# Sharing the first pass over the weights among three chunks of tokens instead of two

## The chip, the cores and the metric

The kernel runs on one core of a Trainium2 chip. The metric is the device time of one execution in microseconds: 958.51 as the median of three runs before the change (957.35 to 958.92). TensorE is written PE below, VectorE DVE, ScalarE ACT, GpSimd POOL, and SyncE, which only issues transfers here, SP.

## The reference

Windowed attention, and behind it a two-layer network with a rational function between the layers:

```python
scores = q @ k.T / sqrt(64)           # 8 batches, 8 heads, 576 positions, 64 wide
mask = (rel >= 0) & (rel < 64)        # rel = query position - key position
attn = softmax(where(mask, scores, -1e9))
x = (attn @ v) as (4608 tokens, 512)
h = x @ w_in                          # 512 x 2048
P = a0 + a1*h + a2*h^2 + a3*h^3
Q = 1 + |b0|*|h| + |b1|*h^2
out = (P / (Q + 1e-6)) @ w_out        # 2048 x 512
```

The weights come in double precision, everything else in float32.

## The kernel before

**Chunks and steps.** The 4608 tokens are nine chunks of 512 (c0 to c8), and the 2048 hidden columns are 16 weight tiles of 128. A step is one chunk with one tile: 12 matmuls for h (`products` of `plan_gate`, L688, called F1 below), a gate on ACT, POOL and DVE (L691 to L733: six DVE operations, of which the first two, L703 and L706, are the last to read h), and 12 matmuls that add to the chunk's output in four PSUM banks (`products` of `plan_out`, L771, called F2). Each product is made of three float32r matmuls: high times low, low times high, high times high. F2 of a step is due three steps (`LAG`) behind its F1. There are 144 steps. h has two PSUM buffers, the gate's temporaries two, its results three.

**Decoding.** Each weight tile comes as double-precision words and is decoded on the chip into a high and a low float32r tile, once for w_in and once for w_out (`plan_decode`): a load of 512 KB, ACT L393, POOL L397, DVE L401 and L406, ACT L417, DVE L420. The decoded tiles stay in SBUF for all chunks. Tiles 8 to 15 are put together in two PSUM banks, b0 and b1.

**Attention.** Each chunk's x is made by four units, one for two heads (`plan_unit`): loads of q, k and v, scores on PE (L527), maxima on DVE, exponentials on ACT, a product on POOL (L589), transposes on PE (L594), the product with v (L608, into one of the two h buffers), and x as high and low tile (L613, L617). c0 and c1 have SBUF buffers of their own, in room that weight tiles take later; from c2 on, a unit uses the buffers `kt`, `w_c`, `vt`, `sm`, `pT` and the banks b0 and b1, which decoding uses too. From chunk `JOIN` on, b0 and b1 are read as one tile. Units of chunks after `PF` have the next unit's scores right behind the product with v.

**Phases.** `phases` (L325) lists (chunk, first tile, tile behind the last). c0 goes over tiles 0 to 7, c1 over all 16, c0 again over 8 to 15, and then each chunk over all. So a tile's decoding is due at its first use: tiles 0 to 7 at steps 0 to 7, tiles 8 to 15 at steps 16 to 23. x has two slots of SBUF. Where a chunk has a phase to come, its partial output goes to memory (`send`, L785) and is added later (L779). If the chunk's x slot has been given away meanwhile, `kept` and `plan_reload` write x to memory and read it back; before the change no chunk needs that.

**Order.** `Plan.order` (L72) simulates the engines with a cost for each operation, and the instructions are written in the order of its start times. Of the operations on an engine that could start within 0.02 us of the first, the one of the lowest rank goes. Ranks are in steps: a gate's is its step, a w_in decode's `need - LI`, its load's `LD` less, a unit's the step that `AH` puts it ahead. `N1` is taken off the rank of L703 and L706. The dictionaries `TILE_AT`, `FETCH_AT`, `UNIT_AT`, `GATE_AT`, `OUT_AT` shift single ranks. SP issues an operation once PE has come within `ahead` steps of its rank.

Of the kernel before, what the change touches and what calls it, by code (L numbers as in the profile page):

```python
# [45 lines left out]
class Plan:  # L46
# [25 lines left out]
    def order(self):  # L72
# [22 lines left out]
        while len(done) < len(self.ops):  # L95
            best = None
            for e in ENGINES:
                able = []
                for op in ready[e]:
                    if e == "SP" and op.rank > now + self.ahead:  # L100
                        continue
                    if any(not slots[s.pool] for s in op.takes):
                        continue
                    t = max([free[e], op.ready + op.late] + [min(slots[s.pool]) for s in op.takes])
                    if op.port:
                        t = max(t, port["POOL" if e == "DVE" else "DVE"])
                    if e == "SP":
                        t = max(t, bus - 2.5)
                    able.append((t, op))
                if not able:  # L110
                    continue
                t0 = min(t for t, _ in able)
                t, op = min(((t, op) for t, op in able if t <= t0 + 0.02), key=lambda x: (x[1].rank, x[0], x[1].n))
                if best is None or t < best[0]:
                    best = t, op
            t, op = best
            for s in op.takes:
                slots[s.pool].remove(min(slots[s.pool]))
                held[s] = len(s.uses)
            cost, e = op.cost, op.engine  # L120
            if e == "PE":
                t += self.TURN.get((last, op.kind), 0.0)
                done_us, at = 0.0, t
                while done_us < cost - 1e-6:
                    w = int((at - self.OFFSET) // self.WINDOW)
                    while seen < w:
                        part = load.get(seen, 0.0) / self.WINDOW
                        fast = part > (0.465 if fast else 0.85)
                        seen += 1
                    slow = 1.0 if fast else self.SLOW[op.kind]  # L130
                    step = min((cost - done_us) * slow, (w + 1) * self.WINDOW + self.OFFSET - at + 1e-6)
                    load[w] = load.get(w, 0.0) + step
                    at += step
                    done_us += step / slow
                cost, last = at - t, op.kind
                now = max(now, op.rank)
            if op.port:
                if e == "DVE" and t == port["POOL"]:
                    cost = 0.55
                port[e] = t + (cost - 0.15 if e == "DVE" else op.port)  # L140
            op.start, op.end = t, t + cost
            if e == "SP":
                bus = max(t, bus) + op.cost
                op.end = bus + 2.0
                free[e] = t + 0.12
            elif e == "PE":
                free[e] = op.end
                op.end += self.DRAIN[op.kind]
            else:
                free[e] = op.end - self.TAIL[e]  # L150
            ready[e].remove(op)
            done.append(op)
            for s, n in list(held.items()):
                if op in s.uses:
                    held[s] -= 1
                    if not held[s]:
                        slots[s.pool].append(max(o.end for o in s.uses) + self.LATENCY)
                        del held[s]
            for o in then.get(op, ()):
                left[o] -= 1  # L160
                if not left[o]:
                    o.ready = max(x.end - self.DRAIN[x.kind] if x.engine == o.engine == "PE" else
                                  x.end + (0.111 if x.kind == "R" and o.engine == "DVE" else self.LATENCY) for x in o.after)
                    ready[o.engine].append(o)
# [16 lines left out]
def swa_rational_ffn(ctx: ExitStack, tc: tile.TileContext, qT, kT, v, w_in, w_out, a, b, out):  # L181
# [7 lines left out]
    NF = DFF // P  # L189
# [12 lines left out]
    tmp = ctx.enter_context(tc.tile_pool(name="tmp", bufs=2))  # L202
    gp = ctx.enter_context(tc.tile_pool(name="gp", bufs=3))
# [90 lines left out]
    w_out_v = w_out.rearrange("(fc p) e -> p fc e", p=P)  # L294

    EC = 2
    PF = 3
    HA = H
    LI, LO = (4, 1.5), (2, 1.5)
    C0R, AH = -12.0, (2, 2, 3.0)  # L300
    TILE_AT = {12: -0.5, 17: -0.5, 18: -2, 20: -1.5, 4: 0.25}
    FETCH_AT = {(0, 2): -0.5, (2, 0): -2, 12: 1}
    UNIT_AT = {(0, 1): 2, (1, 0): -1.5, (2, 0): -0.5}
    GATE_AT = {13: 1, 18: 1.25, 22: -1, 31: 0.25, 33: -0.75, 34: -2, 36: -1}
    OUT_AT = {25: -2, 5: -3}
    UN, GT, F2R, OUTR, N1, SG, LD = 0.3, 0.02, 0.5, -0.5, 0.0, 0, 2.0
    KEEP = 4
    PT_DVE = ((0, 0), (0, 1))
    XH_DVE = ((0, 0), (0, 1))
    LENT = ((0, 1),)  # L310
    MASK_US = 4.8
    PSC = 8
    JOIN = 3
    WC = 2
    ps_b = Early(tc, "ps_b", 1, space=bass.MemoryType.PSUM)
    banks = [ps_b.pool.tile([P, 512], F32, name=f"bank{z}") for z in range(2)]
# [2 lines left out]
    def join():  # L319
        ps_b.close()  # L320
        pool = ctx.enter_context(tc.tile_pool(name="ps_a", bufs=1, space=bass.MemoryType.PSUM))
        span.append(pool.tile([P, 2, 512], F32, name="banks"))
        banks[:] = [span[0][:, z, :] for z in range(2)]

    phases = [(0, 0, 8), (1, 0, NF), (0, 8, NF)]  # L325
    phases += [(c, 0, NF) for c in range(1 + max(c for c, _, _ in phases), NCH)]
    steps = [(c, i) for c, i0, i1 in phases for i in range(i0, i1)]
    total = len(steps)
# [21 lines left out]
    for s, (c, i) in enumerate(steps):  # L350
        need.setdefault(i, s)

    plan = Plan({"w_st": 3, "w_c": WC, "b0": 1, "b1": 1, "kt": 1, "e0": 4, "e1": 2, "sme": 2, "pTe": 2, "sm": 2, "vt": 1, "pT": 1, "h": 2,
                 "tmp": 2, "gp": 3, "o0": 1, "o1": 1, "o2": 1, "o3": 1}, 5.0)
    ready_in, ready_out = {}, {}

    parts = tiles(H, NF)
# [18 lines left out]
    def plan_decode(i, src, his, los, rank, z):  # L376
        in_psum = i >= PSC
        n = 2 * i + z
        plan.shift = TILE_AT.get(n, 0.0)
        home = HOMES[n % len(HOMES)] if n < FROM else "w_st"  # L380
# [41 lines left out]

        plan.shift += FETCH_AT.get(n, 0.0)
        o = plan.add("SP", 1.6, rank - LD, load, uses=[st])
        plan.shift = TILE_AT.get(n, 0.0)
        o = plan.add("ACT", 0.66, rank, scale, [o], [st, sc])
# [20 lines left out]
    def plan_unit(c, hp, rank):  # L447
        early = c < EC
        plan.shift = UNIT_AT.get((c, hp), 0.0)
        if early:  # L450
# [62 lines left out]
        def scores():  # L513
            if c:
                if c >= JOIN and not span:
                    join()
# [12 lines left out]

        joined = c >= JOIN  # L530
        PARTS = [slice(0, NR)] if joined else [slice(z * PR, (z + 1) * PR) for z in range(2)]
# [79 lines left out]
        def x_high():  # L611
            xh[c, hp] = xp.tile([P, CH], F32R, name=f"xh{hp}_{slot_of[first_of[c]]}", bufs=1)
            (nc.vector.tensor_copy if (c, hp) in XH_DVE else nc.scalar.copy)(out=xh[c, hp], in_=u["px"].rearrange("p t s -> p (t s)"))  # L613

# [5 lines left out]
        def link(kind, op):  # L620
            chain[kind] = op
            return op

        r = lambda n: rank + UN * n
        paired = c > PF or c == PF and hp > 0
        ahead = (-2.5 if c > PF else -1 if hp else 2) if c >= PF else 5.5 - hp
        plan.shift += FETCH_AT.get((c, hp), 0.0)
        o = link("load_qk", plan.add("SP", 1.7, r(0) - 2 if early else r(0) + ahead, load_qk, [], [sqk, sq]))
        lv = link("load_v", plan.add("SP", 1.4, r(0) - 1.9 if early else r(0) + ahead + 0.1, load_v, [o], [svt]))
        plan.shift = UNIT_AT.get((c, hp), 0.0)  # L630
        m = [plan.add("PE", 0.51, r(1) - 2, masks, [chain.get("scores")], sps, late=MASK_US if hp == 0 else 0.0, kind="F")] if c == 0 else []
# [18 lines left out]
        link("values", o)  # L650
        oh = plan.add("DVE" if (c, hp) in XH_DVE else "ACT", 0.69 if (c, hp) in XH_DVE else 0.594, r(10), x_high, [o] + free_x.get(c, []), [spx])
        o = plan.add("DVE", 0.688, r(11), x_low, [oh], [spx])
# [24 lines left out]
    def plan_gate(s):  # L677
        c, i = steps[s]
        plan.shift = GATE_AT.get(s, 0.0)
        sh, st, sg = Slot("h"), Slot("tmp"), Slot("gp")  # L680
# [74 lines left out]
    def plan_out(s):  # L755
# [3 lines left out]
        d, sg = gs.pop(s)  # L759
        plan.shift = OUT_AT.get(s, 0.0)  # L760
        if first:
# [114 lines left out]
```

## Time and profile before

| what | value |
|---|---|
| median of three runs | 958.51 us |
| the profiled execution: its own time | 959.0 us |
| the profiled execution: span of the trace | 957.0 us |
| PE busy | 934.6 us, 98% of the span |
| DVE busy | 791.6 us, 83% |
| ACT busy | 669.8 us, 70% |
| POOL busy | 330.7 us, 35% |
| granted TensorE clock, mean | 0.993 |

The span goes from the first to the last instruction. An engine is busy while an instruction of it runs; matmuls overlap, so PE is read from its gaps and from the spacing of starts. Register, branch and DMA-issuing instructions are not counted.

### The profile page before, as it was taken

Reading aid. Unit: us, or ns where it says so; the run is one execution under the profiler, and the core shown is the slowest. Engines: PE = TensorE matmul, PEld = TensorE weight load, DVE = VectorE, ACT = ScalarE, POOL = GpSimd, SP = SyncE. Lnnn points to the kernel's source line nnn. Section 1 sums busy time; section 2 is a strip of 40 time slices with the busy share of each in tenths; the row PEclk is TensorE's granted clock in tenths of the full one; section 3 lists DMA queues with packets and bytes.
Section 4 is the critical chain, followed back from the end, with each engine's and each line's share of the span. In section 5 each row is a group of like instructions: output and inputs, shape, how many; then the busy total and the mean of one; then the engine's idle time right before and its main releaser. Section 6 shows DMA issues by size and latency. Waiting matters only on the chain.

```text
span 957.0 us, 16313 instructions
## 1 busy us (share of the span) xinstructions
PE 934.6 (98%) x6068; PEld 752.0 (79%) x6068; DVE 791.6 (83%) x1198; ACT 669.8 (70%) x1477; POOL 330.7 (35%) x227
## 2 busy tenths in 40 slices
PE   7798999999999999999999999999999999999998
PEld 4576778778888888888888888888888888888886
DVE  5999999999797977887787787887879778777775
ACT  6788777778767577676776677667676676756564
POOL 4756355533323233233323233233132332322221
PEclk9799999999999999999999999999999999999999
DMA  8831323122421112101211121111211121001001
GB/s 301 280 108 45 121 99 113 66 91 85 137 98 44 44 44 71 58 2 54 76 44 44 43 76 54 45 48 48 92 46 46 46 78 35 1 1 45 0 1 45
DMA packets 39103, 66.47 MB, mean 69 GB/s; under 512 B 5616, under 2 KB 22256, under 8 KB 39024
## 3 DMA queue, kind: packets, MB, share of 16 engines
q1 hardware_dynamic: 39024, 65.43, 20.9%
q8 instruction: 48, 0.79, 0.3%
q14 instruction: 31, 0.25, 0.1%
HBM read 54.92 MB, written 10.49 MB: 68 GB/s over the span
## 4 chain that ended last, share of the span: by engine, by line
PE 82%; DVE 11%; issue 2%; DMA 2%; ACT 1%; POOL 0%; SPq 0%; ACTq 0%; DVEq 0%; POOLq 0%
PE o L771 37%; PE h L688 36%; PE ps_x L608 3%; PE banks L527 3%; PE banks L594 2%; DMA w_st<-w_in 2%; DVE gh L720 2%; DVE num L703 1%; DVE gl L733 1%; DVE num L728 1%; DVE u L724 1%; DVE num L706 1%; DVE bank L401 1%; DVE w_c L401 1%; ACT sm L577 1%
## 5 line engine op out<-in xcount | busy, mean ns | idle before, releaser
L710 POOL TENSOR_TENSOR u<-u,ah 128x512 f32<-128x512 f32 x144 | 203.1, 1410 | 422.9 <-ACT u L700 294.9
L688 PE MATMUL h<-xl,wi_h 128*128 128x512 f32 x576 | 230.5, 400 | 4.8 <-DVE num L706 3.2
L771 PE MATMUL o<-wo_h,gl 128*128 128x512 f32 x576 | 231.9, 403 | 0.3 <-ACT ob L783 0.2
L688 PE MATMUL h<-xh,wi_l 128*128 128x512 f32 x576 | 227.8, 396 | 0.0
L688 PE MATMUL h<-xh,wi_h 128*128 128x512 f32 x576 | 227.5, 395 | 0.0
L771 PE MATMUL o<-wo_h,gh 128*128 128x512 f32 x576 | 226.7, 393 | 0.0
L771 PE MATMUL o<-wo_l,gh 128*128 128x512 f32 x576 | 225.8, 392 | 0.0
L713 ACT ACTIVATE ah<-u 128x512 f32<-128x512 f32 x144 | 91.0, 633 | 114.8 <-POOL u L710 114.7
L720 DVE SCALAR_TENSOR_TENSOR gh<-num,a_sb,ah 128x512 fp32r<-128x512 f32 x144 | 111.3, 773 | 49.9 <-ACT ah L716 48.5
L694 ACT ACTIVATE ah<-h 128x512 f32<-128x512 f32 x144 | 85.9, 597 | 81.9 <-PE h L688 56.8
L703 DVE TENSOR_TENSOR num<-num,h 128x512 f32<-128x512 f32 x144 | 98.3, 683 | 45.5 <-ACT num L697 45.3
L688 PEld LDWEIGHTS h<-xl,wi_h 128*128 128x128 f32 x576 | 108.5, 188 | 34.0 <-DVE num L706 4.8
L771 PEld LDWEIGHTS o<-wo_h,gl 128*128 128x128 f32 x576 | 108.2, 188 | 26.9 <-issue 3.1
L688 PEld LDWEIGHTS h<-xh,wi_l 128*128 128x128 f32 x576 | 108.5, 188 | 26.1
L688 PEld LDWEIGHTS h<-xh,wi_h 128*128 128x128 f32 x576 | 108.7, 189 | 24.8
L771 PEld LDWEIGHTS o<-wo_h,gh 128*128 128x128 f32 x576 | 108.1, 188 | 25.2
L771 PEld LDWEIGHTS o<-wo_l,gh 128*128 128x128 f32 x576 | 108.3, 188 | 22.6
L589 POOL TENSOR_TENSOR sm<-sm,rs 128x1024 f32<-128x1024 f32 x36 | 69.8, 1940 | 159.4 <-ACT ah L694 88.1
L728 DVE SCALAR_TENSOR_TENSOR num<-num,a_sb,u 128x512 f32<-128x512 f32 x144 | 115.9, 806 | 2.3
L700 ACT ACTIVATE u<-ah,b_sb 128x512 f32<-128x512 f32 x144 | 117.3, 815 | 0.0
L724 DVE SCALAR_TENSOR_TENSOR u<-u,gh 128x512 f32<-128x512 f32 x144 | 106.2, 738 | 7.1
L697 ACT ACTIVATE num<-h,a_sb 128x512 f32<-128x512 f32 x144 | 111.9, 777 | 0.0
(80 smaller groups left out, 1095.3 us busy)
## 6 DMA issues: line engine op xcount, KB each, us to landing
out<-ob SPq DMA_DIRECT2D x35, 256.0 KB, 2.0
w_st<-w_in SPq DMA_DIRECT2D x16, 512.0 KB, 5.2
w_st<-w_out SPq DMA_DIRECT2D x16, 512.0 KB, 4.1
vt<-v SPq DMA_DIRECT2D x8, 448.0 KB, 5.7
vt<-v SPq DMA_DIRECT2D x8, 384.0 KB, 3.3
vt<-v SPq DMA_DIRECT2D x8, 320.0 KB, 3.9
q<-qT SPq DMA_DIRECT2D x8, 256.0 KB, 4.8
kt<-kT SPq DMA_DIRECT2D x8, 256.0 KB, 4.3
```

Source lines behind the costliest of these rows:

```text
L589: nc.gpsimd.tensor_tensor(out=sm, in0=sm, in1=u["rs"].unsqueeze(2).broadcast_to([P, NR, P]), op=ALU.mult)
L688: nc.tensor.matmul(h, w[i][:, cc, :], x[c, cc], start=n == 0, stop=n == 3 * NCC - 1)
L694: nc.scalar.activation(d["ah"], d["h"], AF.Abs)
L697: nc.scalar.activation(d["num"], d["h"], AF.Identity, scale=a_sb[:, 3:4], bias=a_sb[:, 2:3])
L700: nc.scalar.activation(d["u"], d["ah"], AF.Identity, scale=b_sb[:, 1:2], bias=b_sb[:, 0:1])
L703: nc.vector.tensor_tensor(out=d["num"], in0=d["num"], in1=d["h"], op=ALU.mult)
L710: nc.gpsimd.tensor_tensor(out=d["u"], in0=d["u"], in1=d["ah"], op=ALU.mult)
L713: nc.scalar.activation(d["ah"], d["u"], AF.Ln, bias=QADD)
L720: nc.vector.scalar_tensor_tensor(out=d["gh"], in0=d["num"], scalar=a_sb[:, 0:1], in1=d["ah"], op0=ALU.add, op1=ALU.mult)
L724: nc.vector.scalar_tensor_tensor(out=d["u"], in0=d["u"], scalar=QADD, in1=d["gh"].bitcast(F32), op0=ALU.add, op1=ALU.mult)
L728: nc.vector.scalar_tensor_tensor(out=d["num"], in0=d["num"], scalar=a_sb[:, 0:1], in1=d["u"], op0=ALU.add, op1=ALU.subtract)
L771: nc.tensor.matmul(acc[t], g[:, ts], w[i], start=first and n == 0, stop=last and n == 2)
```

## The change

The list of phases becomes: c0 over tiles 0 to 7, c1 over 0 to 9, c2 over all 16, c1 over 10 to 15, c0 over 8 to 15, and then c3 to c8 over all. Three things follow from existing code. Tiles 8 and 9 are due at steps 16 and 17, tiles 10 to 15 at steps 28 to 33. c2's attention is due at step 18 instead of 32, and c2's x takes the slot of c0's, so c0's eight x tiles (256 KB each) go to memory and come back for step 40; c1 has a partial output that is stored and added as c0's is. Chunk 3 is read with two separate banks and without pairing (`JOIN` and `PF` go from 3 to 4). The planner's constants are other ones.

```diff
-                t, op = min(((t, op) for t, op in able if t <= t0 + 0.02), key=lambda x: (x[1].rank, x[0], x[1].n))
+                t, op = min(((t, op) for t, op in able if t <= t0 + 0.05), key=lambda x: (x[1].rank, x[0], x[1].n))
...
-    PF = 3
+    PF = 4
     HA = H
-    LI, LO = (4, 1.5), (2, 1.5)
-    C0R, AH = -12.0, (2, 2, 3.0)
-    TILE_AT = {12: -0.5, 17: -0.5, 18: -2, 20: -1.5, 4: 0.25}
-    FETCH_AT = {(0, 2): -0.5, (2, 0): -2, 12: 1}
-    UNIT_AT = {(0, 1): 2, (1, 0): -1.5, (2, 0): -0.5}
-    GATE_AT = {13: 1, 18: 1.25, 22: -1, 31: 0.25, 33: -0.75, 34: -2, 36: -1}
-    OUT_AT = {25: -2, 5: -3}
-    UN, GT, F2R, OUTR, N1, SG, LD = 0.3, 0.02, 0.5, -0.5, 0.0, 0, 2.0
+    LI, LO = (1.5, 1.25), (2, 4)
+    C0R, AH = -12, (5, 0, 2)
+    TILE_AT = {22: 0.25, 7: -0.25}
+    FETCH_AT = {17: -0.5}
+    UNIT_AT = {(1, 1): -2, (2, 1): 0.5}
+    GATE_AT = {0: -1, 17: -0.25, 20: -0.25}
+    OUT_AT = {}
+    UN, GT, F2R, OUTR, N1, SG, LD = 0.1, 0.1, 0.25, -1.75, 3.5, 0, 4
     KEEP = 4
     PT_DVE = ((0, 0), (0, 1))
-    XH_DVE = ((0, 0), (0, 1))
+    XH_DVE = ((0, 0),)
...
-    JOIN = 3
+    JOIN = 4
...
-    phases = [(0, 0, 8), (1, 0, NF), (0, 8, NF)]
+    phases = [(0, 0, 8), (1, 0, 10), (2, 0, NF), (1, 10, NF), (0, 8, NF)]
...
-                 "tmp": 2, "gp": 3, "o0": 1, "o1": 1, "o2": 1, "o3": 1}, 5.0)
+                 "tmp": 2, "gp": 3, "o0": 1, "o1": 1, "o2": 1, "o3": 1}, 3.0)
```

The last number is `ahead`.

## Rows read from the trace of the kernel before

**Rows 1.** The page: busy time of the engines over the span, and the granted TensorE clock in 40 slices, in tenths of full speed.

```profile
PE 934.6 (98%) x6068; PEld 752.0 (79%) x6068; DVE 791.6 (83%) x1198; ACT 669.8 (70%) x1477; POOL 330.7 (35%) x227
...
PEclk9799999999999999999999999999999999999999
```

**Rows 2.** Busy time of each engine in five stretches. The columns: the stretch and its length, then PE, PE's weight loads, DVE, ACT and POOL with their instructions, the granted clock, the DMA share and GB/s.

```profile
17.60:26.60 9.00, 4.58 (x80) 3.84 (x80) 7.80 (x16) 6.51 (x27) 7.18 (x5) 1.00 0.96 345
26.60:94.30 67.70, 58.73 (x513) 46.02 (x513) 65.07 (x102) 56.70 (x143) 43.55 (x27) 0.90 0.43 140
94.30:111.10 16.80, 16.80 (x72) 13.63 (x73) 16.80 (x28) 11.58 (x19) 4.52 (x3) 1.00 0.25 95
111.10:199.40 88.30, 87.72 (x375) 69.60 (x374) 87.79 (x139) 65.73 (x110) 45.74 (x31) 1.00 0.27 90
199.40:252.00 52.60, 52.60 (x514) 42.02 (x513) 47.21 (x80) 44.12 (x130) 18.65 (x12) 1.00 0.38 118
```

**Rows 3.** The same view for single lines, between 111.1 and 199.4 us: F1's matmuls (L688; PE and its weight loads), F2's (L771), a gate's last DVE operation (L733, one for a gate) and a decode's last (L420, one for half a tile pair). The fifth row is L733 between 199.4 and 252 us, the sixth L420 between 26.6 and 94.3.

```profile
111.10:199.40 88.30, 44.96 (x183) 33.97 (x183) 1.00 0.27 90
...
111.10:199.40 88.30, 47.46 (x192) 35.64 (x191) 1.00 0.27 90
...
111.10:199.40 88.30, 10.86 (x16) 1.00 0.27 90
...
111.10:199.40 88.30, 10.21 (x15) 1.00 0.27 90
...
199.40:252.00 52.60, 5.14 (x7) 1.00 0.38 118
...
26.60:94.30 67.70, 9.11 (x13) 0.90 0.43 140
```

**Rows 4.** PE in order of time between 47 and 95 us: start, length, line, operation, and in brackets the idle time before it and what ended it. The second and third row are two matmuls in a row of the same F1.

```profile
47.81 0.50 PE L688 MATMUL h<-xl,wi_h 128*128 128x512 f32 x1 [2.23 <-DVE num L706]
...
49.45 0.63 PE L688 MATMUL h<-xh,wi_l 128*128 128x512 f32 x1
49.87 0.63 PE L688 MATMUL h<-xl,wi_h 128*128 128x512 f32 x1
...
59.25 1.15 PE L608 MATMUL ps_x<-pT,vt 128*64 128x64 f32 x32 [0.89 <-DVE num L706]
...
62.60 1.15 PE L608 MATMUL ps_x<-pT,vt 128*64 128x64 f32 x32 [0.61 <-DVE xl L617]
...
79.22 0.49 PE L688 MATMUL h<-xl,wi_h 128*128 128x512 f32 x1 [0.75 <-DVE num L706]
...
88.58 1.15 PE L608 MATMUL ps_x<-pT,vt 128*64 128x64 f32 x32 [0.55 <-ACT bank L393]
...
94.29 0.50 PE L688 MATMUL h<-xl,wi_h 128*128 128x512 f32 x1 [1.61 <-DVE xl L617]
```

**Rows 5.** DVE in order of time: the last operation of two gates in a row. Nine operations start from the first to before the second: six of gates and three of decoding.

```profile
149.35 0.67 DVE L733 TENSOR_TENSOR gl<-num,ah 128x512 fp32r<-128x512 f32 x1
...
154.93 0.67 DVE L733 TENSOR_TENSOR gl<-num,ah 128x512 fp32r<-128x512 f32 x1
```

**Rows 6.** Groups of instructions: the DVE operation that makes the gate's high part between 26.6 and 94.3 us, and the same between 94 and 200 us. Busy time and mean ns of one stand behind the bar, then the idle time before. Last, one such operation in the chain of waits: start, length.

```profile
L720 DVE SCALAR_TENSOR_TENSOR gh<-num,a_sb,ah 128x512 fp32r<-128x512 f32 x6 | 7.2, 1207 | 0.5 <-ACT ah L716 0.5
...
L720 DVE SCALAR_TENSOR_TENSOR gh<-num,a_sb,ah 128x512 fp32r<-128x512 f32 x19 | 14.5, 762 | 0.1
...
53.80 2.31 DVE gh L720
```

**Rows 7.** Groups of instructions between 199.4 and 252 us: the maxima of the attention, one for a unit.

```profile
L568 DVE TENSOR_REDUCE nmx<-sm 128x8 f32<-128x1024 f32 x5 | 6.1, 1213 | 0.1
```

**Rows 8.** SP's issue of the first weight load, and the loads of one unit in the list of DMA issues: size, and us to landing.

```profile
8.05 0.33 SPq L387 DMA_DIRECT2D w_st<-w_in  x1
...
vt<-v SPq DMA_DIRECT2D x8, 448.0 KB, 5.7
...
q<-qT SPq DMA_DIRECT2D x8, 256.0 KB, 4.8
kt<-kT SPq DMA_DIRECT2D x8, 256.0 KB, 4.3
```

**Rows 9.** The chain of waits between 200 and 260 us, in order of time: start, length, what. All of it is PE. The first row is the first scores of c2, the last c2's first F1.

```profile
201.96 1.03 PE bank L527 x32
...
221.13 1.08 PE ps_x L608 x32
222.21 0.90 PE o L771 x3
223.11 0.87 PE bank L594 x8
...
233.27 0.69 PE o L771 x3
...
250.28 1.03 PE banks L527 x32
251.31 0.89 PE o L771 x3
252.20 2.79 PE h L688 x12
```

**Rows 10.** Single lines over the whole span: who waited for the copies that empty the output banks (L783; us, times), and the landing time of the 256 KB stores (L790).

```profile
  PE o L771: 0.2, 1
...
DMA to landing us min/median/max: 1.7/2.0/3.3
```

## The prediction

> **What bounds the kernel now.** I read the shares of the engines first [rows 1]: PE at 98% of the span with the clock down only in the first two fortieths, so nearly all that can be won lies early. The stretches [rows 2] then show three regimes. Up to 94.3 us PE is held: between 26.6 and 94.3 it is busy 58.73 of 67.70, at a mean clock of 0.90, beside a DVE that is busy 65.07. From 94.3 to 199.4 us both are full: PE 104.5 of 105.1, DVE 104.6. From 199.4 PE alone is full. A loss behind 94 us could therefore only be a new one, and a gain has to come from the 9.0 us that PE stands before it and from the clock.
>
> What PE waits for there is in its order of time [rows 4]: twice L706, which gives back an h buffer (2.23 and 0.75 us), and four times for the attention of c1, its product with v or the h buffer that this product holds (0.89, 0.61, 0.55, 1.61). After the 2.23 us the next F1 runs part of its way with starts 0.43 us apart (49.45 to 49.87), where the full stretch has 87.72 us for 375 matmuls [rows 2], 0.234 each: the lower clock level. Some 8 of the 12 matmuls have it, 8 x 0.20 = 1.6 us. Together these are 6.6 + 1.6 = 8.2 us.
>
> Why could the order of the work not simply be made better there? DVE's prices say it. Between two ends of gates lie 154.93 - 149.35 = 5.58 us and nine operations [rows 5], 0.62 each: a gate (six) is 3.72 us, half a tile pair of decoding (three) 1.86. Check: between 111.1 and 199.4 us end 16 gates and 15 halves [rows 3], 16 x 3.72 + 15 x 1.86 = 87.4, and DVE was busy 87.79. A step is 24 matmuls on PE, 24 x 0.234 = 5.61. So for steps 8 to 23, with tiles 8 to 15 due in them, DVE needs 16 x 3.72 + 16 x 1.86 = 89.3 us and PE 16 x 5.61 = 89.8. There is no slack: had PE come to step 8 earlier, DVE would have made it wait afterwards. DVE's work up to 199 us is what sets the end, and PE's early gaps only show it.
>
> **The change part by part.**
>
> *Decoding later, c2 earlier.* Out of steps 8 to 23 go six tiles, 12 halves or 22.3 us of DVE; in come four units of c2. Their price: between 199.4 and 252 us DVE is busy 47.21 [rows 2], seven gates take 26.0, and 21.2 are left for four to five units [rows 3, 7], 4.5 each. Steps 8 to 17 then cost DVE 37.2 + 7.4 (two tiles) + 18.0 = 62.6 us, and PE 56.1 + four units of about 3.2 (1.03 + 0.87 + 1.08 and turns [rows 9]) = 68.9. Steps 18 to 33 cost DVE 59.5 + 22.3 = 81.8 and PE 89.8. DVE now has 6 and 8 us to spare, where it had none. By itself this is worth nothing, as PE is full there; it allows the front to be shorter.
>
> *The front.* Three edits use it: N1 = 3.5 puts L703 and L706 ahead of other DVE work, which is the wait of 2.23 and 0.75; c1's units come three steps earlier, into PE's idle time, which is the other four waits; LI = 1.5 decodes w_in tiles later beside them. At most all 8.2 us go. DVE sets a limit: from 26.6 to 111.1 us it does 81.9 us of work, of which about 5 (L703 and L706 of two steps, 2.5, and tile 8's first operations, 2.5) aren't needed by the eighth F2, and it idles 2.6; so the front can be shorter by 5 to 8. At least nothing is won: the order changes and DVE's sum does not. It can also be a loss, priced among the rivals. I take half of 8.2, 4.1 us: the first wait and its clock are cured by N1 alone (3.8), and the rest is shared with what DVE then owes.
>
> *Loads.* The ranks put two units of c1, some 960 KB each [rows 8], ahead of the first weights, issued at 8.05 us now. At 345 GB/s [rows 2] that is 5.6 us. The first F1 comes some 30 us later [rows 4] and DVE has attention to do until then, so I take 0; without this cover 5.6.
>
> *x out and back.* Eight tiles of 256 KB go out and eight come in, 4.2 MB or 12 us at 345 GB/s, while the queues run at 90 to 118 GB/s [rows 2]; a store lands in 2.0 us [rows 10]. It costs no engine anything but SP its issues. Coming back, the loads have from the end of c2's F1 to step 40, six steps or 34 us, for 6.1 + 4 us. Going out, c2's x tiles wait for the stores, and these aren't issued before PE is at step 11 (rank 14, `ahead` 3). I take 0; the upper end is a rival.
>
> *A second partial output.* Four more ACT copies and four more DVE additions (one operation, 0.62 each) lie in slack behind step 18. One more change of the output banks: at all of them together PE waited 0.2 us once [rows 10], so +0.2, between 0 and 0.2.
>
> *c3 unpaired.* Where other products follow scores or a product with v, three matmuls of F2 take 0.89 or 0.90 instead of 0.69 [rows 9]; a pair pays these 0.2 us once, separated ones twice. Three units: +0.6. c3's separate banks make an operation of 1024 columns into two of 512, in the slack of DVE and ACT: 0, or 1 us were it not there.
>
> Sum: -4.1 + 0.2 + 0.6 = -3.3. The profiled execution took 959.0 us (span 957.0), 0.5 above the median of the runs: 955.7 on its scale, 955.2 against the median.
>
> **The rivals.**
>
> *More is won.* With the lead DVE has, N1 lets all of the 8.2 us go: 959.0 - 8.2 + 0.8 - 0.5 = 951.1. For it: the slack of 6 and 8 us. Against it: DVE's limit of 5 to 8, of which N1 itself spends 2.5.
>
> *The front gains nothing.* POOL and DVE get into each other's way: L720 takes 1.207 us in the front and 0.762 later, one of them 2.31 [rows 6]. With LI = 1.5 more decoding lies among the gates. Three more meetings at 2.31 - 0.76 = 1.55 are 4.6 us, which takes the 4.1 away: 959.0 + 0.5 + 0.8 - 0.5 = 959.8; without the meetings but with an order no better, 959.3. Against it: two of c1's POOL products leave the gates' stretch for the time before it. The Trainium skill has a rule for this (SBUF — State Buffer, "Who interferes with whom"): a VectorE instruction with two SBUF inputs contends with a GpSimd instruction that reads SBUF, and the later one waits until the other is done. The length of 2.31 us agrees.
>
> *c2 is late* (slower). Before, from c2's first scores to its first F1 went 252.20 - 201.96 = 50.2 us [rows 9]. Now there are seven steps and four units for it, from step 11, where the stores may go, to step 18: 39.3 + 12.8 = 52 us. The eight stores need 6.1 + 2.0 = 8 of these before the first x tile can be written, and ACT, which writes the x tile, holds gates behind that wait. If the units keep the old pace behind the stores, c2's x is 6 us late. F2 of the three steps before covers up to 8.4 us, but the gates then run dry as well. From the point where the last unit ends more than 8.4 us late, PE stands; I price it at 6 us and two F1 at the lower clock, 2 x 1.6: 955.2 + 9.2 = 964.4. Against it: the old pace was that of a full DVE, and the new stretch has 6 us of slack. The Trainium skill's clock gate rule (TensorE: Matmul & The Clock Gate, "HAM oscillation — how this bites in real kernels") says that matmuls after a long enough wait run at half clock; the rows on the 2.23 us agree, and if the clock stayed up, this rival would be 961.2.
>
> **How the numbers follow.** The forecast gets 0.47, all 8.2 us 0.13, no gain 0.20, c2 late 0.20. From 950.5 to 962.5 us lie the forecast, no gain, most of the better case and the lighter half of the late one, 8 in 10. A run can tell 0.2% from no change, 1.9 us: faster is under 956.6, slower over 960.4. The forecast lies below 956.6 in 0.40 of its 0.47; faster 0.53. No gain gives most of its part to no change: 0.21 with the rest of the forecast. Slower 0.26.
>
> **What would show it.** Right: PE idle before 94 us falls from 9.0 in that stretch to about 5, no PE wait on L706 of over 1 us, the eighth F2 starts 3 to 5 us before 111.1, and PE is full from there on, across c2's first F1 and step 40. DVE has idle time between steps 8 and 34. Wrong: the eighth F2 comes no earlier (no gain), L720 above 1.2 us in the front (the shared port), a PE wait of several us on c2's x or behind a store (c2 late), or one at step 40 on the x read back, for which I have kept nothing.

## The result and the profile after

The changed kernel takes 963.75 us (median of four runs, 962.96 to 964.31), the kernel before 958.71 beside it (957.35 to 959.62). The ratio is 1.0052, with a 95% interval of 1.0037 to 1.0067: slower by 5.0 us, where 3.3 less was forecast. The profiled execution took 963.37 us, its span is 961.6 (957.0 before), its mean granted clock 0.990 (0.993).

The page of the kernel after, the same lines as in [rows 1]:

```profile
PE 936.8 (97%) x6068; PEld 752.4 (78%) x6068; DVE 791.1 (82%) x1209; ACT 672.7 (70%) x1482; POOL 337.5 (35%) x227
...
PEclk8999999999999999999999999999999999999999
```

The stretches of the kernel after, with the columns of [rows 2]. The eighth F2 starts at 113.58 here, at 111.11 before. Between 26.6 us and the eighth F1 PE stands 68.70 - 57.68 = 11.0 us, where it stood 9.0 before.

```profile
17.60:26.60 9.00, 5.74 (x72) 4.64 (x68) 5.01 (x13) 6.43 (x26) 6.57 (x4) 0.81 0.92 329
26.60:95.30 68.70, 57.68 (x503) 44.49 (x499) 62.65 (x100) 54.91 (x140) 40.83 (x25) 0.93 0.46 159
95.30:113.60 18.30, 17.52 (x73) 13.43 (x74) 18.30 (x29) 12.75 (x21) 9.76 (x7) 1.00 0.00 0
113.60:156.00 42.40, 40.48 (x342) 31.34 (x341) 40.52 (x72) 34.50 (x91) 14.26 (x10) 1.00 0.48 154
156.00:260.00 104.00, 103.95 (x511) 84.21 (x511) 95.82 (x149) 78.93 (x142) 49.51 (x32) 1.00 0.27 88
```

A comparison needs the same state of PE's work in both. One is the start of the eighth F1 (F1 no. 8 below), with all of c0's and c1's attention done. The stretch up to it, before and after:

```profile
0.00:94.28 94.28, 76.07 (x740) 57.70 (x740) 81.34 (x139) 72.55 (x214) 57.45 (x47) 0.93 0.55 186
```

```profile
0.00:95.20 95.20, 77.16 (x740) 58.09 (x740) 76.89 (x135) 70.84 (x212) 54.34 (x45) 0.91 0.56 196
```

PE has the same 740 instructions behind it, 94.28 - 76.07 = 18.2 us idle before and 18.0 after. DVE has done 4.4 us less (76.89 against 81.34): the decoding did move out. PE got nothing for it; it arrives 1.0 us later (F1 no. 8 at 95.32 instead of 94.29). Four runs below are edited only behind this front: in them and the kernel after F1 no. 8 starts between 94.50 and 96.16, in the kernel before and the one run with its front at 94.29 and 93.45. So the front is about 1 us later, and no gain. The other 3.6 us come between there and the end (957.0 - 94.3 = 862.7, and 961.6 - 95.3 = 866.3). PE in order of time, kernel after, its waits from 47 us on:

```profile
47.53 0.50 PE L688 MATMUL h<-xl,wi_h 128*128 128x512 f32 x1 [3.59 <-DVE num L706]
...
57.42 0.50 PE L771 MATMUL o<-wo_h,gl 128*128 128x512 f32 x1 [0.71 <-DVE gl L733]
...
80.12 0.80 PE L771 MATMUL o<-wo_h,gl 128*128 128x512 f32 x1 [2.52 <-DVE gl L733]
...
90.79 0.50 PE L771 MATMUL o<-wo_h,gl 128*128 128x512 f32 x1 [0.51 <-DVE gl L733]
...
95.32 0.47 PE L688 MATMUL h<-xl,wi_h 128*128 128x512 f32 x1 [0.20 <-DVE num L706]
...
110.67 0.50 PE L688 MATMUL h<-xl,wi_h 128*128 128x512 f32 x1 [0.69 <-DVE num L706]
...
120.11 0.47 PE L771 MATMUL o<-wo_h,gl 128*128 128x512 f32 x1 [0.78 <-ACT wi_h L417]
...
123.73 0.50 PE L688 MATMUL h<-xl,wi_h 128*128 128x512 f32 x1 [0.62 <-DVE num L706]
...
155.76 0.50 PE L688 MATMUL h<-xl,wi_h 128*128 128x512 f32 x1 [0.52 <-DVE xl L617]
```

The wait for the third F1, which N1 was to cure, is 3.59 here, 2.23 before [rows 4]; in the four runs with the same front it is 2.49 to 3.59. The waits at the product with v are gone. In their place F2 waits three times for the end of a gate (L733), 3.7 us in all, and the one of 2.52 is 2.50 to 2.52 in all five traces. Up to F1 no. 8 this list comes to 7.5 us, [rows 4] to 6.6. Behind 95.3 us PE stands 2.8 us up to its last product, 2.6 of it in the last four waits; before, it stood 0.6 in all of that time (88.30 - 87.72 in [rows 2]). That is 2.2 of the 3.6; of the remaining 1.4, 1.1 are PE's busy time (turns between kinds of product, as I take it) and 0.3 the end. Behind 156 us PE waits no more, neither at c2's first F1 (173.6 us) nor at step 40.

What happened to the first loads: SP's first issue of a weight load is at 16.89 us, where it was 8.05 [rows 8]. SP, ACT and DVE in order of time, kernel after:

```profile
16.89 1.30 SPq L387 DMA_DIRECT2D w_st<-w_in  x2
...
22.27 0.67 ACT L393 ACTIVATE w_c<-w_st 128x512 f32<-128x512 f32 x1 [1.03 <-DMA w_st<-w_in]
...
23.99 0.66 ACT L393 ACTIVATE w_c<-w_st 128x512 f32<-128x512 f32 x1 [1.04 <-DMA w_st<-w_in]
...
24.55 0.57 ACT L613 CAST xh<-ps_x 128x512 fp32r<-128x512 f32 x1
...
25.16 0.69 DVE L617 TENSOR_TENSOR xl<-ps_x,xh 128x512 fp32r<-128x512 f32 x1 [3.40 <-ACT xh L613]
```

ACT stands for the weights, with the cast of c0's x queued behind them (L613), and DVE stands 3.40 us for that cast. DVE between 20 and 32 us, before and after, is busy 10.85 and 6.58 of 12 us:

```profile
20.00:32.00 12.00, 6.22 (x80) 5.13 (x80) 10.85 (x18) 7.89 (x23) 10.48 (x7) 0.84 0.94 339
20.00:32.00 12.00, 6.43 (x82) 5.34 (x82) 6.58 (x13) 7.63 (x20) 8.97 (x6) 0.85 0.97 375
```

My cover for the late weights was DVE's attention, and that attention stood behind the weights.

### The profile page after: what moved, and what is told of

Same layout as the page of the kernel before. It is cut to its first block, busy times and chain, and to the rows that moved or that the text cites. A ratio compares the mean times of both kernels' runs of the same rounds, so it can differ in the third digit from the quotient of the medians.

```text
span 961.6 us, 16400 instructions
## 1 busy us (share of the span) xinstructions
PE 936.8 (97%) x6068; PEld 752.4 (78%) x6068; DVE 791.1 (82%) x1209; ACT 672.7 (70%) x1482; POOL 337.5 (35%) x227
## 4 chain that ended last, share of the span: by engine, by line
PE 87%; DVE 7%; ACT 3%; DMA 2%; issue 1%; SPq 1%; POOL 0%; DVEq 0%; POOLq 0%; ACTq 0%
PE o L771 39%; PE h L688 38%; PE ps_x L608 3%; PE banks L527 2%; PE banks L594 2%; PE bank L527 1%; DVE gh L720 1%; DMA w_st<-w_in 1%; DMA kt<-kT 1%; DVE u L724 1%; DMA vt<-v 1%; ACT sm L577 1%; PE bank L594 1%; DVE w_c L406 1%; DVE num L728 1%
## 5 line engine op out<-in xcount | busy, mean ns | idle before, releaser
L710 POOL TENSOR_TENSOR u<-u,ah 128x512 f32<-128x512 f32 x144 | 208.2, 1446 | 420.5 <-ACT u L700 282.8
L771 PE MATMUL o<-wo_h,gl 128*128 128x512 f32 x576 | 232.1, 403 | 4.6 <-DVE gl L733 3.7
L688 PE MATMUL h<-xl,wi_h 128*128 128x512 f32 x576 | 230.9, 401 | 5.6 <-DVE num L706 5.1
L688 PE MATMUL h<-xh,wi_l 128*128 128x512 f32 x576 | 227.8, 396 | 0.0
L688 PE MATMUL h<-xh,wi_h 128*128 128x512 f32 x576 | 227.3, 395 | 0.0
L771 PE MATMUL o<-wo_h,gh 128*128 128x512 f32 x576 | 227.2, 395 | 0.0
L771 PE MATMUL o<-wo_l,gh 128*128 128x512 f32 x576 | 226.7, 393 | 0.0
L720 DVE SCALAR_TENSOR_TENSOR gh<-num,a_sb,ah 128x512 fp32r<-128x512 f32 x144 | 109.4, 761 | 60.3 <-ACT ah L716 57.7
L694 ACT ACTIVATE ah<-h 128x512 f32<-128x512 f32 x144 | 85.9, 597 | 97.4 <-PE h L688 52.5
L771 PEld LDWEIGHTS o<-wo_h,gl 128*128 128x128 f32 x576 | 108.6, 189 | 34.0 <-DVE gl L733 5.2
L688 PEld LDWEIGHTS h<-xl,wi_h 128*128 128x128 f32 x576 | 108.4, 188 | 32.8 <-DVE num L706 7.0
L703 DVE TENSOR_TENSOR num<-num,h 128x512 f32<-128x512 f32 x144 | 98.4, 683 | 42.9 <-ACT num L697 42.9
L688 PEld LDWEIGHTS h<-xh,wi_l 128*128 128x128 f32 x576 | 108.5, 188 | 25.9
L771 PEld LDWEIGHTS o<-wo_h,gh 128*128 128x128 f32 x576 | 108.4, 188 | 25.2
L688 PEld LDWEIGHTS h<-xh,wi_h 128*128 128x128 f32 x576 | 108.6, 189 | 24.2
L771 PEld LDWEIGHTS o<-wo_l,gh 128*128 128x128 f32 x576 | 108.7, 189 | 23.1
L697 ACT ACTIVATE num<-h,a_sb 128x512 f32<-128x512 f32 x144 | 111.6, 775 | 0.0
```

Of the source, the lines that this page charges most:

```text
L688: nc.tensor.matmul(h, w[i][:, cc, :], x[c, cc], start=n == 0, stop=n == 3 * NCC - 1)
L694: nc.scalar.activation(d["ah"], d["h"], AF.Abs)
L697: nc.scalar.activation(d["num"], d["h"], AF.Identity, scale=a_sb[:, 3:4], bias=a_sb[:, 2:3])
L703: nc.vector.tensor_tensor(out=d["num"], in0=d["num"], in1=d["h"], op=ALU.mult)
L710: nc.gpsimd.tensor_tensor(out=d["u"], in0=d["u"], in1=d["ah"], op=ALU.mult)
L720: nc.vector.scalar_tensor_tensor(out=d["gh"], in0=d["num"], scalar=a_sb[:, 0:1], in1=d["ah"], op0=ALU.add, op1=ALU.mult)
```

## The experiments

All are compared with the kernel before, run beside them. "A" is a kernel made from the one after, "B" from the one before. A number after a ratio is the difference of medians.

**First look: is it the late weights, and does the front's gain stay?**

A, weights first. SP issues the first three w_in loads ahead of c1's first two units:

```diff
+        first = [w_load[n] for n in (0, 2, 4)]
+        at = min(ops.index(o) for o in u_load[1, 0] + u_load[1, 1])
+        ops[at:at] = first
```

> The changed kernel with one edit: SP issues the first three loads of w_in ahead of c1's first two units, where the changed kernel issues them behind. The order on every other engine stays. Theory A (the weights come too late: ACT waits for them with c0's x behind it, and DVE idles 4.9 us that it owes until step 17): that idle time goes, the eighth F2 starts 2 to 4 us before 113.6, and the time falls by 2 to 4 us, to 960 to 962. Theory B (the loss is the new order of DVE's and PE's own work; the loads only move idle time about): within 1 us of 963.75.

964.03 us, 1.0037 to 1.0067: no change against 963.75. DVE's idle time before 60 us hardly moves (60 - 42.97 = 17.0 us, 17.1 without the edit), and F1 no. 8 starts at 96.01; the idle time only lies elsewhere. I take it that this is because the rest of the order was made for late weights.

B, the opposite edit: c1's first two units' loads ahead of the first weight load.

```diff
+        first = u_load[1, 0] + u_load[1, 1]
+        at = ops.index(w_load[0])
+        ops[at:at] = first
```

> The kernel before with one edit: SP issues the loads of c1's first two units (q, k and v) ahead of the first weights, as the changed kernel does. The order on every other engine stays. Theory A (late weights are the loss of the front): 2 to 4 us slower, 961 to 963, with DVE idle 4 to 5 us more before 40 us. Theory B (the order of DVE's work is): under 1 us slower.

964.12 us, 1.0038 to 1.0072, +5.1. DVE in order of time has one long wait that the kernel before has not, for exponentials that stand behind the weights in ACT's queue (the first row is ACT, the second DVE):

```profile
23.44 0.66 ACT L393 ACTIVATE w_c<-w_st 128x512 f32<-128x512 f32 x1 [5.32 <-DMA w_st<-w_in]
...
26.92 0.68 DVE L584 SCALAR_TENSOR_TENSOR sums<-sums,zero 128x8 f32<-128x8 f32 x1 [5.62 <-ACT sm L577]
```

In an order not made for it, the late loads cost 5.1 us, near the 5.6 that I had priced "without this cover". In A the cost, if it is there, can't be taken back by the loads alone.

B, front relief: the low word of the decode (L406) is left out for tiles 0 to 7, 16 operations of 0.62 us [rows 5] or 9.9 us of DVE's work. In the kernel before 13 of them start ahead of F1 no. 8, the last three at 94.8, 97.9 and 106.6 us.

```diff
+            if i < 8:
+                return
             nc.vector.scalar_tensor_tensor(out=c, in0=d["w"][:, :, 0], ...
```

> The kernel before without the third decoding step (L406, the low word's bits) of tiles 0 to 7: 16 DVE operations, 9.9 us, are left out, all before 110 us; the weights of these tiles lack their lowest bits. The order of all else stays. As the prediction had it (DVE has no slack between steps 8 and 23, so PE would be made to wait there for whatever it wins in front): 0 to 2 us faster, and PE idle 3 to 6 us between 94 and 200 us. The rival (the front is a bound of its own, and what it wins stays won): 4 to 8 us faster, 951 to 955, with PE idle under 1.5 us from there to 200.

955.66 us, 0.9951 to 0.9977, -3.3. F1 no. 8 starts at 92.04 instead of 94.29, and behind the front PE stays full, the second row:

```profile
26.60:92.00 65.40, 54.60 (x506) 42.27 (x500) 57.58 (x90) 55.76 (x142) 43.78 (x27) 0.97 0.42 138
92.00:200.00 108.00, 107.65 (x484) 85.79 (x488) 106.18 (x167) 78.31 (x132) 51.53 (x34) 1.00 0.27 88
```

So a gain in the front is kept with little slack in steps 8 to 23: DVE idles 108.00 - 106.18 = 1.8 us there, about what the three late operations would have taken. My argument said that DVE would take the gain back. The test has a limit: DVE too comes to step 8 with less to do, so it doesn't show what PE would keep if it alone came earlier.

B, relief everywhere: `if i < 8` becomes `if True`.

> The kernel before without that step (L406) in all 16 tiles: 32 DVE operations, 19.8 us, half of them between 94 and 199 us; all weights lack their lowest bits. As the prediction had it: now the middle has its slack and the front's win stays, 4 to 8 us faster, clearly under the run with tiles 0 to 7 alone. The rival: the same time as that run, within 1 us, since the middle never bound.

955.11 us, 0.9946 to 0.9976: 0.5 us beyond front relief alone. Nearly 10 us of slack in the middle are worth next to nothing on top of it.

```profile
91.80:200.00 108.20, 108.09 (x493) 87.26 (x494) 101.78 (x153) 79.23 (x134) 51.37 (x34) 1.00 0.27 88
```

**Second look: the wait on L706 and the store of x.**

ACT in order of time shows what stands ahead of the first gate (kernel after; the first of 16 exponentials, the last, then the gate):

```profile
39.46 0.37 ACT L577 ACTIVATE sm<-bank,nmx 128x128 f32<-128x128 f32 x1 [0.85 <-PE h L688]
...
42.12 0.24 ACT L577 ACTIVATION_READ_ACCUMULATOR sm<-bank,nmx 128x1 f32 x1
42.22 0.63 ACT L694 ACTIVATE ah<-h 128x512 f32<-128x512 f32 x1
```

The exponentials of a unit of c1 hold ACT for 2.8 us. On DVE a decode and the unit's maxima (44.67 to 46.73 us) then come between L703 and L706, in spite of N1. A and B, the first gate early: L694 and L697 of step 0 go ahead of these exponentials, L706 right behind L703.

```diff
+        last = max((o for o in exps_of if ops.index(o) < ops.index(a0)), key=ops.index)
+        at = max(ops.index(last), ops.index(f1[0]) + 1)
+        ops[at:at] = [a0, n0]
+        ops.insert(ops.index(n1) + 1, n2)
```

> The changed kernel with the first gate's first operations moved: ACT makes L694 and L697 of step 0 ahead of the 16 exponentials of a c1 unit instead of behind them, and DVE makes L706 of step 0 right behind its L703 instead of behind a decode step and c1's maxima. Theory C (PE's 3.59 us wait for the third F1 is put down to L706, but what holds it is the order of ACT's and DVE's queues): that wait falls under 1 us, the lower clock behind it goes too, and the time falls by 1 to 3 us. Theory D (DVE's amount of work is the bound of the front, PE only waits elsewhere): the wait goes and as much comes back before step 8; within 1 us of 963.75.

A: 967.12 us, 1.0080 to 1.0116, 3.4 above the kernel after. The four executions lie between 965.19 and 969.33; the trace is of the shortest. PE in order of time:

```profile
44.81 0.50 PE L689 MATMUL h<-xl,wi_h 128*128 128x512 f32 x1 [0.24 <-DVE num L707]
...
50.18 0.63 PE L594 MATMUL bank<-ident_r,sm 128*128 128x128 f32 x4 [2.30 <-issue]
51.53 0.66 PE L594 MATMUL bank<-ident_r,sm 128*128 128x128 f32 x4 [0.73 <-ACT sm L577]
...
59.01 0.51 PE L772 MATMUL o<-wo_h,gl 128*128 128x512 f32 x1 [1.59 <-DVE gl L734]
```

The wait on L706 (here L707) goes from 3.59 to 0.24. Behind it stand 2.30 and 0.73 us at the transposes of the attention that the gate was moved past, and the first F2's wait for its gate (here L734) is 1.59 instead of 0.71. F1 no. 8 starts at 96.96, 1.6 us later than in the kernel after.

> The same move in the kernel before, where the third F1 waits 2.23 us. Theory C: that wait goes with its clock, 1 to 3 us faster, 955.7 to 958. Theory D: within 1 us of before.

B: 959.97 us, 1.0007 to 1.0028, +1.2; the wait falls to 0.24, and 2.25 us come back at the transposes. That trace is of the longest of eight executions, 962.86. A wait that is 2.23 or 3.59 us long gave nothing when it was taken away by this edit alone.

A, front relief: the edit of B's front relief.

> The changed kernel without L406 of tiles 0 to 7 (16 DVE operations, 9.9 us; the weights of these tiles lack their lowest bits), as was done to the kernel before, which gained 3.3 us. Theory E (DVE comes to step 8 owing some 4 us, and this owing is PE's 2.1 us of waits between 95 and 156 us): these waits fall under 0.7 us and the gain is larger than in the kernel before, 4 to 7 us. Its rival (those waits come from c2's attention or its wait for the stores): they stay, and the gain is 2 to 4 us.

961.12 us, 1.0016 to 1.0036, 2.6 below the kernel after. The row below is this kernel between 95 and 156 us, where PE stands 61.00 - 58.62 = 2.38 us. The waits behind the front stay.

```profile
95.00:156.00 61.00, 58.62 (x422) 45.73 (x421) 58.53 (x99) 46.43 (x117) 23.25 (x15) 1.00 0.34 112
```

A, every x tile stored twice:

```diff
+                    twin = tc.dram_tile([P, CH], F32, name=f"y{c}_{hp}_{k}")
+                    nc.sync.dma_start(out=twin, in_=x[c, hp].bitcast(F32))
```

> The changed kernel with each of the eight stores of c0's x issued twice, the second into another place of memory: 2.1 MB more, 6 us at 345 GB/s, before c2's x may be written. If the way out is covered: within 1 us of 963.75. If c2's attention waits for the stores: 2 to 6 us slower, with PE waits on c2's x or behind it between 115 and 175 us.

968.50 us, 1.0090 to 1.0121, 4.8 above the kernel after. PE then waits for the loads of c2's k, which stand in SP's queue behind the stores:

```profile
134.53 0.45 PE L527 MATMUL bank<-kt,q 64*64 64x128 f32 x8 [1.76 <-DMA kt<-kT]
...
136.07 1.46 PE L527 MATMUL bank<-kt,q 64*64 64x128 f32 x24 [1.09 <-DMA kt<-kT]
```

The kernel after has no such wait. One way out for x may be free, a second is not; the next look takes the one away.

**Third look: the trip alone, and whether the constants or the phases matter.**

A, one store of eight; the reads fetch that one tile.

```diff
+                    if (hp, k) != (0, 0):
+                        x_part[c, hp, k] = x_part[c, 0, 0]
+                        return
```

> The changed kernel with one of the eight stores of c0's x made instead of eight; all eight loads read that one tile, so the second half of c0's output is computed from a wrong x. The order stays. If the way out to memory holds c2's attention up (doubling it cost 4.8 us): 1 to 3 us faster than 963.75, and PE waits between 105 and 156 us fall under 1 us. If only the doubled number was too much for the queue: within 1 us.

963.41 us, 1.0034 to 1.0060: no change. The way out costs nothing (the eight reads are still made), and PE's waits between 95 and 156 us aren't its work either:

```profile
95.00:156.00 61.00, 58.62 (x417) 44.92 (x415) 59.09 (x100) 48.05 (x113) 24.34 (x17) 1.00 0.25 79
```

The phases of the change with other constants (besides the lines shown, single shifts, `KEEP`, `JOIN`, `XH_DVE` and `ahead` differ):

```diff
-    LI, LO = (1.5, 1.25), (2, 4)
-    C0R, AH = -12, (5, 0, 2)
+    LI, LO = (4.75, -3.5), (3.25, 1.25)
+    C0R, AH = -12, (2.5, -1.0, 1.5)
...
-    UN, GT, F2R, OUTR, N1, SG, LD = 0.1, 0.1, 0.25, -1.75, 3.5, 0, 4
+    UN, GT, F2R, OUTR, N1, SG, LD = 0.4, 0.04, 1.75, -17.75, 0.5, 0, 6.5
```

> The phases of the changed kernel (three chunks over 8, 10 and 16 tiles, x to memory and back) with other constants for the order: the w_in decodes of tiles 0 to 7 4.75 steps ahead again (the changed kernel has 1.5), those of tiles 8 to 15 3.5 behind, c1's units at 2.5 steps ahead instead of 5, the stores of x at 10 steps ahead instead of 4, and some single shifts. Theory F (the phases are worth what the prediction said, about 3 us, and the changed kernel's constants lose it in front): 2 to 6 us faster than before, 952.5 to 956.5, and clearly faster than the same search over the old phases. Theory G (the phases are worth nothing by themselves, and the loss is that of the constants): as fast as the same search over the old phases, within 1.5 us.

967.46 us, 1.0074 to 1.0102.

The phases of the kernel before with other constants, `LI, LO = (4, 1.75), (2.0, 3.25)`, `AH = (2, 0.0, 2.5)`, `PF = 4`, and again single shifts and the like:

> The control: the phases of the kernel before (two chunks) with constants found in the same way and with about as much search. Theory F: 0 to 2 us faster than before, and 2 us or more behind the three-chunk version. Theory G: within 1.5 us of the three-chunk version.

961.02 us, 1.0012 to 1.0028. One list of phases gives 963.8 and 967.5 us, the other 958.7 and 961.0, by such constants alone. Neither theory foresaw this: the three-chunk list was slower both times, by 5.0 and 6.4 us. That speaks against the phases, but two sets of constants each don't separate them from their constants, and the change's phases with the constants of before were not tried.

**Fourth look: where is the slack?**

L406 twice for tiles 8 to 15, 9.9 us more of DVE's work from step 8 on, in B and in A.

```diff
+            for _ in range(2 if i >= 8 else 1):
                 nc.vector.scalar_tensor_tensor(out=c, in0=d["w"][:, :, 0], ...
```

> The kernel before with L406 of tiles 8 to 15 made twice (the second time changes nothing): 16 more DVE operations, 9.9 us, between 94 and 199 us, where DVE is busy 99%. Reading H (the middle has no DVE slack, as the prediction worked out: DVE 89.3 us beside PE's 89.8): 6 to 10 us slower, with PE waits of that size between 95 and 200 us. Reading I (DVE only looks full there, since decoding fills it ahead of need): under 3 us slower.

> The same edit in the changed kernel: 4 of the 16 operations (2.5 us) fall to tiles 8 and 9 before step 18, 12 (7.4 us) to tiles 10 to 15, decoded beside steps 18 to 33. As the prediction worked out (6 us to spare up to step 17, 8 behind): under 3 us slower than 963.75, and under half of what the kernel before loses by it. If the change gave DVE no slack: 6 to 10 us slower here too.

B: 969.91 us, 1.0108 to 1.0142, +11.3. A: 974.14 us, 1.0149 to 1.0180, +10.4 against 963.75. Both pay in full; the slack that I had counted for A takes nothing off. The stretch 95 to 200 and 200 to 260 us, kernel after:

```profile
95.00:200.00 105.00, 102.07 (x665) 80.18 (x665) 96.25 (x156) 81.14 (x181) 44.02 (x29) 1.00 0.33 110
200.00:260.00 60.00, 60.00 (x261) 48.81 (x260) 58.69 (x94) 45.04 (x74) 29.82 (x19) 1.00 0.22 69
```

The same for A with L406 twice:

```profile
95.00:200.00 105.00, 100.39 (x654) 78.44 (x655) 96.13 (x156) 79.87 (x177) 41.94 (x27) 1.00 0.32 107
200.00:260.00 60.00, 55.77 (x235) 43.21 (x234) 59.66 (x96) 41.09 (x66) 32.09 (x19) 1.00 0.17 59
```

In the kernel after DVE does idle, 105.00 - 96.25 = 8.75 us, but beside c2's attention, before the decodes of tiles 10 to 15 are due. From 190 us on it is full:

```profile
156.00:190.00 34.00, 33.95 (x209) 27.31 (x209) 27.20 (x41) 26.24 (x56) 13.75 (x10) 1.00 0.23 72
190.00:260.00 70.00, 70.00 (x304) 56.90 (x303) 68.62 (x109) 52.69 (x87) 35.76 (x23) 1.00 0.28 96
```

With L406 twice PE stands 60.00 - 55.77 = 4.2 us between 200 and 260. In the idle stretch DVE did no more than before (96.13 against 96.25).

A, middle relief: `if i >= 8: return` ahead of L406.

> The changed kernel without L406 of tiles 8 to 15 (16 DVE operations; those weights lack their lowest bits). PE's new waits between 95 and 156 us are 2.1 us more than before. If DVE's amount of work makes them (tile 8 and 9 are 2.5 us of it less): they fall by 1 us or more, and the time by 1 to 2.5 us. If single places in the order of the queues make them: they stay within 0.5 us, and the time within 1 us of 963.75.

963.36 us, 1.0035 to 1.0065, -0.4. PE's waits between 95 and 156 us stay, 61.00 - 58.52 = 2.48:

```profile
95.00:156.00 61.00, 58.52 (x418) 45.45 (x417) 58.13 (x97) 47.22 (x112) 24.77 (x17) 1.00 0.34 108
```

## Why the prediction was wrong, and where it was right

**The step that failed: the front, -4.1.** It measured +1.0 to the same state of work. The first wait, which N1 alone was to cure, stayed, and other waits took the place of those at c1's attention. Three things were wrong in the step.

First, the premise that DVE's missing slack in steps 8 to 23 holds the front back, so that slack there "allows the front to be shorter". The sum of gates and halves against 24 matmuls a step was right as a sum: PE and DVE are both full there. But the kernel after has slack there and its front is no shorter, and more slack (A, middle relief) gave 0.4 us. B's front relief won 3.3 us and kept them with DVE idle only 1.8 us of 108, and relief of the middle added 0.5. So a stretch in which two engines are just even takes an earlier start of both; whether PE's alone would be kept was not tested. Against more work DVE's full stretch is a limit, as B with L406 twice shows (+11.3).

Second, "the first wait and its clock are cured by N1 alone (3.8)". The row names L706 as releaser, and L706 is only the last link: ahead of it stand 16 exponentials in ACT's queue, and a decode and maxima in DVE's. N1 moves the ranks of L703 and L706 alone; L694 and L697, which feed them, stay behind the exponentials on ACT, and the decode and the maxima came between L703 and L706 all the same. Taking the wait away by an edit gave +3.4 in A and +1.2 in B. I had counted PE's idle rows as if each could be had alone. The four that I put down to c1's attention name L706, L617 twice and a decode's L393 as releasers [rows 4], so they too are ends of queues. In A all but 0.2 us of c1's four did go, and F2 waits 3.7 us for gates instead, beside a DVE that has no pause from 66 to 84 us. That some of the 8.2 could be had is shown only for less work: 9.9 us off DVE gave 3.3.

Third, the clock is no gain either: to the same state its mean is 0.93 before and 0.91 after, and to 95 us 0.91 to 0.95 in the five traces with the new front, so a change of that size can't be told. That the 3.59 us are followed by the lower level is seen in the spacing of starts of this F1, 0.23 at first and 0.43 from 49.14 us on. Most of the front's lower clock doesn't lie behind that wait either: in the kernel before the mean is 0.58 between 30 and 40 us.

```profile
49.14 0.63 PE L688 MATMUL h<-xl,wi_h 128*128 128x512 f32 x1
49.56 0.63 PE L688 MATMUL h<-xh,wi_h 128*128 128x512 f32 x1
```

**Loads, 0.** The step named two covers: the first F1 comes late anyway, and "DVE has attention to do until then". The second failed. The queue that matters is ACT's: its wait for the weights holds the cast of c0's x, and DVE behind it idles 5.4 us between 20 and 32 us, where it idled 1.2. B with c1's loads first paid 5.1 of the 5.6 us named without cover. How much of it A pays is open, as giving the weights back alone won nothing.

**The four waits between 95 and 156 us, +2.2 net, stood in no step.** They aren't the stores (A with one store) and aren't cured by 9.9 us less of DVE's work for the first eight tiles (A's front relief). Middle relief doesn't test DVE's load there well: only tiles 8 and 9 are decoded in that stretch, and DVE was busy 58.13 us of it all the same. They name three releasers (L706 twice, L417, L617), so I take them for places where single operations stand in the wrong order; that is argued, not shown, and what would cure them stays open.

**Right.** The turns and the second partial output, +0.8: what is left of the later 3.6 us when the waits are taken off is 1.4, some 0.3 of it at the end, so about 1.1 for them, by subtraction only. x out and back, 0: A with one store takes the same time, and step 40 waits for nothing. Of the slack of 6 and 8 us the first was there: from step 8 to step 18 DVE idles 75.30 - 69.07 = 6.2 us, from there to step 34 86.80 - 82.85 = 4.0.

```profile
98.20:173.50 75.30, 72.57 (x538) 56.30 (x537) 69.07 (x117) 59.13 (x143) 28.12 (x19) 1.00 0.31 99
173.50:260.30 86.80, 86.80 (x377) 70.52 (x377) 82.85 (x129) 65.04 (x107) 43.83 (x28) 1.00 0.29 96
```

But it is a sum over a stretch: most of it lies where DVE has nothing due, and the six tiles that were moved come in time only with DVE full behind it.

**The rivals.** "The front gains nothing" came nearest in its cause, with 959.3 for an order no better. Of the 4.5 us missing from it 1.0 arose up to F1 no. 8 and 2.2 in the waits behind it. Its mechanism, the meetings of POOL and DVE, didn't come: L720 takes 860 ns in the front, 1207 before.

```profile
L720 DVE SCALAR_TENSOR_TENSOR gh<-num,a_sb,ah 128x512 fp32r<-128x512 f32 x6 | 5.2, 860 | 1.1 <-ACT ah L716 1.1
```

The rule of the Trainium skill that I had named for it (SBUF — State Buffer, "Who interferes with whom") may hold for the one of 2.31 us before; here the longest took 1.47, and the rule decided nothing. "c2 is late" gave almost the measured time, 964.4, by another cause: PE is full across c2's first F1. The stores are not far from a limit, though: doubling them made c2's k late and cost 4.8 us.

## What to carry to other kernels

Before a cost is moved away from an engine, take a little of its work out at the place in question and see whether the time follows: here 9.9 us less in the front gave 3.3 us, and 9.9 us less in the middle on top of it gave 0.5. A wait's releaser is the last link of several in-order queues, so read what stood ahead of it on each of them before pricing its cure, and expect that a wait which is moved away by itself may come back one place later, as it did in both kernels here. A slack found as a sum over a stretch is worth something only if it lies after the operands are there and before the work is due.

## What was not expected of the hardware

The granted clock of the front is not a property of the order. The kernel after and the run with one store have the same order up to F1 no. 8; the rows are these two, to 95 us:

```profile
0.00:95.00 95.00, 77.04 (x740) 58.09 (x740) 76.69 (x134) 70.84 (x212) 54.13 (x45) 0.91 0.57 196
0.00:95.00 95.00, 74.36 (x737) 55.98 (x738) 76.32 (x133) 70.05 (x211) 53.16 (x45) 0.95 0.56 193
```

The second has the higher clock and idles more, 20.6 us against 18.0, and it reaches F1 no. 8 no earlier (96.16 against 95.32). Whole executions say the same: in the 48 of the kernel before that were run beside the experiments the mean clock goes from 0.988 to 0.996, and the time does not follow it (958.1 to 958.8 us at 0.988, 957.9 to 959.3 at 0.996). So a trace's idle time and its lost clock should not be added as two losses that a better order would both give back, as I did with 6.6 + 1.6: in the two rows one stands in the place of the other. That other engines set PE's pace there is my reading of it, not shown by these rows alone.
